# A fused attention and two-MLP kernel: a deeper read-ahead of the second MLP's weights, another order inside a slot, and constant products between the attention steps

## The chip, the cores and the metric

The kernel runs on one core of one Trainium2 chip. The metric is the time on the device in microseconds (us), from the start to the end of one execution; inputs lie in device memory (HBM) before it starts.

## The reference

Four batches, eight heads, 576 positions, head size 64, everything in float32. Attention comes first, causal within a window of 128 positions with a bias that grows with distance; its output, as 2304 tokens of 512 numbers, goes through a first MLP, a root-mean-square norm and a gated second MLP:

```python
scores = scale * np.matmul(q, k.transpose(0, 1, 3, 2))
scores = np.where(mask, scores + bias[None], -1000000000.0)
attn = np.exp(scores - np.max(scores, axis=-1, keepdims=True))
attn = attn / (np.sum(attn, axis=-1, keepdims=True) + 1e-09)
x = np.matmul(attn, v)                      # 2304 x 512 after the heads are put side by side
...
h = x @ w_in                                # 512 x 2048
x = (h * np.clip(h + 3.0, 0.0, 6.0) / 6.0) @ w_out
...
xn = x / np.sqrt(np.mean(x * x, axis=-1, keepdims=True) + 1e-06) * rms_g
g, val = xn @ w_gate, xn @ w_val            # 512 x 1536 each
out = (g / (1.0 + np.exp(-g)) * val) @ w_out
```

The weights of both MLPs are float64 in HBM.

## The kernel before, in words

Tokens are cut into 18 tiles of 128 and the tiles into six blocks of three. Heads are worked on in pairs, so one *pair* is a block and two heads, and one *step* (`Step`) is one tile of 128 queries of a pair against its 256 keys. Scores go through TensorE (`scores`), then VectorE adds the bias and finds the maximum (`bias`), ScalarE takes the exponential (`exp`), GpSimd inverts the sum (the last two lines of `exp`), VectorE multiplies by it (`divide`), TensorE transposes the result (`transpose`), ScalarE copies it out of PSUM (`weights`) and TensorE multiplies with the values (`values`). After a pair's last step `Pair.finish` splits the result into two float32r parts, which is how the MLPs read it. The stages of one step are spread over four positions of a software pipeline: at position `t` the code works on scores, bias and exp of step `t` (`cur`), on the division of step `t-1` (`mid`), on the transposes of step `t-2` (`old`) and on the values of step `t-3` (`done`).

The first `AHEAD` = 15 positions run attention alone (loop at L486), preceded by 50 transposes of a constant (L483). After them come *slots* (loop at L564): in each, one tile of 128 of the first MLP's 2048 hidden numbers is computed for a block (`product1`, 12 matmuls), the activation is applied and split (L586, L587, L592, L597), the attention stream goes on by one step, and the second product (`product2`, called in `finish1`, 9 matmuls) of the slot before is added up. There are 96 slots before the second MLP, in seven parts (`PARTS`); block 0 is split into two parts so that block 1 can come between.

Weights are converted on the chip from float64 words into two float32r parts (`convert`, a generator in six stages on ScalarE and VectorE). The first MLP's 16 units are loaded and converted by `First` in the late steps and in the first 15 slots (parts 0 and 1). The second MLP's 36 tiles go through `Second`: `load` issues the DMA of one raw tile, `begin` does the first three stages of a conversion, `finish` the rest, and the result is stored to a DRAM scratch (`kept`), from which GpSimd's queue fetches it for the second MLP. Raw tiles have two buffers. `finish` is called once a slot in part 3 from its fourth slot on, and in three slots of four in parts 4 and 5.

When a block's last slot is over, `Norm` takes over its three output tiles: `square` (ScalarE and GpSimd) finds the factor `ri`, `front` at the start of a slot multiplies a tile by it and copies the transposes of an earlier tile out of PSUM (`yt`), and `back`, at a slot's end, issues four transposes (`ps_x`) and the next `square`. `ps_x` and the attention's transposes share one PSUM buffer (tag `T`).

Each engine works its instructions off in the order in which the code issues them (`manual_schedule`), so a waiting instruction holds everything behind it on that engine. The DMAs of SP are such a queue too. The lines that matter here, in a slot of the kernel before:

```python
for x in norms:
    x.front()                                  # L568
...
if mid:
    mid.divide()                               # L583
act.activation(r[:, :nq], ps[:, :nq], AF.Relu, bias=three)   # L586
```

and in `Second.finish`:

```python
self.load()                                    # L199
...
self.done += 1
self.begin()                                   # L206
```

Of the kernel before, what the change touches and what calls it, by code (L numbers as in the profile page):

```python
# [14 lines left out]
U64 = mybir.dt.uint64  # L15
# [5 lines left out]
P = 128  # L21
# [3 lines left out]
DM = H * D  # L25
# [12 lines left out]

WARM = 50
PARTS = [(0, 0, CUT), (1, 0, M1), (0, CUT, M1)] + [(b, 0, M1) for b in range(2, len(BLOCKS))]  # L40
# [15 lines left out]
def f32(ap):  # L56
    return ap.bitcast(F32)
# [3 lines left out]
def fused_kernel(ctx: ExitStack, tc: tile.TileContext, qd, kd, v, w1, w2, rms_g, out):  # L61
# [29 lines left out]
    def make_constants():  # L91
        make_identity(nc, ident)

        pool.iota(rel, pattern=[[-1, 2 * P]], base=P, channel_multiplier=1, allow_small_or_imprecise_dtypes=True)
        pool.affine_select(out=rel, in_=rel, compare_op=ALU.is_ge, fill=BIG, base=P, pattern=[[-1, 2 * P]], channel_multiplier=1)
        pool.affine_select(out=rel, in_=rel, compare_op=ALU.is_ge, fill=BIG, base=WINDOW - 1 - P, pattern=[[1, 2 * P]], channel_multiplier=-1)
        pool.memset(half, -0.5)
        pool.memset(minus, -1.0)
        vec.memset(three, 3.0)
        for h in range(H):  # L100
            vec.memset(qscale[h % 2 * D : (h % 2 + 1) * D, h // 2 : h // 2 + 1], -float(2 ** (h + 1)) / np.sqrt(D))
        pool.tensor_copy(rel_split, rel)
        pool.memset(rel_split[HALF:, : P + HALF], BIG)
# [66 lines left out]
    class Second:  # L170


        def __init__(self):
            self.n, self.loaded, self.done, self.raw, self.run = 3 * M2, 0, 0, None, None
            self.kept = [dram.tile([P, 2, 2, DM], F32, tag=f"w2_{i}", name=f"w2_{i}") for i in range(self.n // 2)]
            self.pairs = []

        def load(self):
            i = self.loaded
            self.raw = None  # L180
            if i < self.n:
                self.raw = wcpool.tile([P, DM], U64, tag="w", name="wraw", bufs=2)
                sp.dma_start(out=self.raw, in_=w2[i // 3, :, (i % 3) * DM : (i % 3 + 1) * DM])
                self.loaded += 1

        def begin(self):

            if self.raw is not None:
                self.run = convert(self.raw, DM, wcpool, 1, vec)
                for _ in range(3):  # L190
                    next(self.run)

        def finish(self):

            if self.run is None:
                return
            run, self.run = self.run, None
            next(run)
            self.load()  # L199
            t = wcpool.tile([P, 2, DM], F32R, tag="wt", name="w", bufs=1)  # L200
            run.send(t)
            next(run)
            i = self.done
            sp.dma_start(out=self.kept[i // 2][:, i % 2], in_=f32(t))
            self.done += 1
            self.begin()  # L206

# [212 lines left out]
    class Norm:  # L420
# [24 lines left out]

        def front(self):
            t = self.t
            if t < self.n:
                vec.tensor_scalar(self.y[t], self.y[t], self.ri[t], None, ALU.mult)
            if t - 2 in self.ps:  # L450
                k = t - 2
                yt = ypool.tile([P, KC, P], F32, tag="yt", name="yt", bufs=2)
# [29 lines left out]
    warm = ps_h.tile([P, 4 * P], F32, tag="h", name="warm")  # L482
    for i in range(WARM):  # L483
        pe.transpose(warm[:, i % 4 * P : (i % 4 + 1) * P], ident, ident)
    pairs[0].scale()
    for t in range(AHEAD):  # L486
# [4 lines left out]
        if done:  # L491
            done.values()
        if mid:
            mid.divide()
        if old:
            old.weights()
        cur.bias()
        cur.exp()
        if done and done.last:
            done.pair.finish()  # L500
        prepare(cur)
        if t == 2:
# [45 lines left out]
    for p, (b, m0, m1) in enumerate(PARTS):  # L548
# [15 lines left out]
        for m in range(m0, m1):  # L564
            t, slot = slot, slot + 1
            cur, mid, old, done = [stream.get(t - i) for i in (0, 1, LAG, LAG + 1)]
            for x in norms:
                x.front()  # L568
            if p == 3 and m == 2:
                first.close()  # L570
                wcpool = second.enter_context(tc.tile_pool(name="wcpool", bufs=1, side="right", **OPEN))
                W2.load()
                W2.begin()
            ps = ps_h.tile([P, 4 * P], F32, tag="h", name="ps_h")
# [5 lines left out]
            if done:  # L580
                done.values()
            if mid:
                mid.divide()  # L583
            g = gpool.tile([P, 2, 3 * P], F32R, tag="g", name="g")
# [3 lines left out]
            if old:  # L588
                old.weights()
            if cur:  # L590
                cur.bias()
            act.copy(g[:, 0, :nq], r[:, :nq])  # L592
            if cur:
                cur.exp()
            if done and done.last:
                done.pair.finish()
            vec.tensor_sub(g[:, 1, :nq], r[:, :nq], f32(g[:, 0, :nq]))  # L597
            prepare(cur)
            between(mid)
            if p < 2:  # L600
                k = m + 1 if p == 0 else CUT + 1 + m
                W1.load(k + 3)
                if k < M1:
# [3 lines left out]
                    W1.step(k, 5)  # L607
            if not last and (p == 3 and m > 2 or p > 3 and m % 4 != 3):
                W2.finish()
# [25 lines left out]
    for b, (_, n) in enumerate(BLOCKS2):  # L635
        nq = n * P
        xs, xs2 = xs2, []
        for m in range(M2):
            for x in norms:
                x.front()  # L640
            ps_g = ps_a.tile([P, 4 * P], F32, tag="S0", name="ps_g") if m % 2 else ps_h.tile([P, 4 * P], F32, tag="h", name="ps_g")
# [64 lines left out]
```

## Time and profile before

| | us |
|---|---|
| median of 3 runs | 1069.63 (1067.77 to 1069.94) |
| the profiled execution, its own time | 1070.02 |
| its span, first to last instruction | 1068.1 |
| TensorE busy in the span | 1031.7 (97%) |
| VectorE busy | 459.6 (43%) |
| ScalarE busy | 434.4 (41%) |
| GpSimd busy | 103.8 (10%) |
| granted TensorE clock, mean (1.0 is 2.4 GHz) | 0.971 |

In the profile PE is TensorE's matmuls, PEld its weight loads, DVE VectorE, ACT ScalarE, POOL GpSimd and SP the engine whose queue issues most DMAs. All times inside a profile are counted from the start of the span. PE's busy time is that of records whose ends are modelled, so a stretch with PE busy throughout is not a stretch at PE's peak: the granted clock and the length of equal pieces of work tell more. The whole span has three stages: constants and the 15 attention steps to 55 us, the slots to 609 us, the second MLP to the end.

### The profile page before, as it was taken

How to read it: one execution, taken by the hardware profiler on the slowest of the kernel's cores; microseconds unless marked ns; L12 is line 12 of the kernel's file. 1: busy time of each engine (PE TensorE's matmuls, PEld its weight loads, DVE VectorE, ACT ScalarE, POOL GpSimd, SP SyncE). 2: the span in 40 equal slices, each digit the busy share in tenths (PEclk: the TensorE clock that was granted, in tenths of full speed). 3: DMA queues.
4: the chain of work that ended last, by engine and by line, in shares of the span. 5: the costliest groups of instructions: out<-in, count | busy, mean ns of one | idle time of the engine just before them, and what ended most of it. 6: DMA issues, size and time to landing. Idle time of an engine off the chain costs nothing.

```text
span 1068.1 us, 14589 instructions
## 1 busy us (share of the span) xinstructions
PE 1031.7 (97%) x5678; PEld 895.2 (84%) x5678; DVE 459.6 (43%) x1096; ACT 434.4 (41%) x952; POOL 103.8 (10%) x219
## 2 busy tenths in 40 slices
PE   7899999999999799989999999999999999999998
PEld 5477778888777588878899899999999999999997
DVE  3578774345576666767632322212212222222212
ACT  3679864355555556656532332112112112112111
POOL 2322011121111111111121010000000000000000
PEclk7599999999999999999999999999999999999999
DMA  6154500003565455444459720010100100100000
GB/s 207 55 212 185 224 28 28 29 29 97 188 202 192 166 166 186 163 165 142 145 193 305 250 71 11 11 49 1 60 1 1 60 1 1 60 1 1 30 1 30
DMA packets 49237, 105.28 MB, mean 99 GB/s; under 512 B 3856, under 2 KB 28432, under 8 KB 44816
## 3 DMA queue, kind: packets, MB, share of 16 engines
q1 hardware_dynamic: 46576, 85.47, 23.8%
q0 software_dynamic: 2592, 18.88, 5.2%
q8 instruction: 44, 0.72, 0.3%
q14 instruction: 25, 0.20, 0.1%
HBM read 76.02 MB, written 28.31 MB: 98 GB/s over the span
## 4 chain that ended last, share of the span: by engine, by line
PE 55%; ACT 0%; issue 0%; DVE 0%; ACTq 0%
PE ps_o L412 20%; PE ps_g L399 14%; PE ps_v L399 14%; PE ps_h L399 6%; PE ps_av L355 0%; PE ps_t L342 0%; PE ps_x L465 0%; PE ps_s L293 0%; DVE y L632 0%; ACT wx L123 0%; DVE xs L541 0%; ACT xs L540 0%; ACT junk L441 0%; ACT t L586 0%; DVE t L587 0%
## 5 line engine op out<-in xcount | busy, mean ns | idle before, releaser
L412 PE MATMUL ps_o<-w,g 128*128 128x512 f32 x1512 | 390.9, 402 | 5.7 <-DVE w L134 2.9
L412 PEld LDWEIGHTS ps_o<-w,g 128*128 128x128 f32 x1512 | 279.5, 190 | 71.6 <-issue 9.6
L399 PE MATMUL ps_h<-xs,w 128*128 128x384 f32 x1152 | 222.8, 341 | 7.9 <-DVE t L587 7.6
L399 PEld LDWEIGHTS ps_h<-xs,w 128*128 128x128 f32 x1152 | 205.0, 190 | 18.4 <-DVE t L587 11.7
L647 DVE TENSOR_TENSOR t<-t,ps_v 128x384 f32<-128x384 f32 x72 | 39.9, 554 | 306.0 <-PE ps_v L399 306.0
L399 PE MATMUL ps_g<-xs,w 128*128 128x384 f32 x864 | 163.8, 337 | 0.5 <-ACT xs L540 0.3
L399 PE MATMUL ps_v<-xs,w 128*128 128x384 f32 x864 | 161.6, 334 | 0.0
L399 PEld LDWEIGHTS ps_g<-xs,w 128*128 128x128 f32 x864 | 153.1, 188 | 7.4 <-ACT xs L540 0.7
L399 PEld LDWEIGHTS ps_v<-xs,w 128*128 128x128 f32 x864 | 151.0, 188 | 0.0
L644 ACT ACTIVATE t<-ps_g 128x384 f32<-128x384 f32 x72 | 35.4, 492 | 196.6 <-PE ps_g L399 196.6
L649 ACT CAST g<-t 128x384 fp32r<-128x384 f32 x72 | 36.9, 513 | 156.6 <-DVE t L647 156.6
L586 ACT ACTIVATE t<-ps_h,three 128x384 f32<-128x384 f32 x96 | 55.3, 576 | 103.3 <-PE ps_h L399 102.9
L587 DVE SCALAR_TENSOR_TENSOR t<-t,ps_h 128x384 f32<-128x384 f32 x96 | 52.9, 551 | 85.1 <-ACT t L586 85.1
L328 ACT ACTIVATE t<-t,m 128x256 f32<-128x256 f32 (+1 forms) x144 | 69.4, 483 | 27.2 <-DVE m L316 27.2
L592 ACT CAST g<-t 128x384 fp32r<-128x384 f32 x96 | 49.4, 514 | 44.3 <-DVE t L587 42.4
L597 DVE TENSOR_TENSOR g<-t,g 128x384 fp32r<-128x384 f32 x96 | 53.4, 556 | 26.0 <-ACT g L592 25.7
L342 PE MATMUL ps_t<-ident,t 128*128 128x128 f32 x272 | 50.0, 310 | 12.8 <-ACT yt L453 8.7
L134 DVE TENSOR_TENSOR w<-wx,w 128x512 fp32r<-128x512 f32 (+1 forms) x52 | 44.5, 857 | 34.2 <-ACT w L132 34.2
L330 POOL TENSOR_SCALAR r<-den 128x2 f32<-128x2 f32 x72 | 21.7, 301 | 386.0 <-ACT t L328 386.0
L336 DVE TENSOR_SCALAR t<-t,r 128x256 f32<-128x256 f32 (+1 forms) x144 | 42.4, 337 | 39.0 <-POOL r L331 37.3
L132 ACT CAST w<-wx 128x512 fp32r<-128x512 f32 (+1 forms) x52 | 39.1, 751 | 47.1 <-issue 27.0
L650 DVE TENSOR_TENSOR g<-t,g 128x384 fp32r<-128x384 f32 x72 | 40.2, 558 | 41.7 <-ACT g L649 41.7
(63 smaller groups left out, 742.4 us busy)
## 6 DMA issues: line engine op xcount, KB each, us to landing
wraw<-w SPq DMA_DIRECT2D x36, 512.0 KB, 4.4
w<-w SPq DMA_DIRECT2D x36, 512.0 KB, 3.2
w<-w POOLq DMA_DIRECT2D x18, 1024.0 KB, 5.3
wraw<-w SPq DMA_DIRECT2D x16, 1024.0 KB, 7.8
kraw<-kd SPq DMA_DIRECT2D x20, 256.0 KB, 2.7
vraw<-v SPq DMA_DIRECT2D x20, 256.0 KB, 4.0
qraw<-qd SPq DMA_DIRECT2D x24, 192.0 KB, 2.9
x<-yt SPq DMA_DIRECT2D x18, 256.0 KB, 2.7
```

What stands on the lines that cost most here:

```text
L134: vec.tensor_sub(t[:, 1], x, f32(t[:, 0]))
L328: act.activation(p, p, AF.Exp, bias=self.m[:, a : a + 1], scale=-1.0, accum_out=self.den[:, a : a + 1])
L336: vec.tensor_scalar(p, p, self.r[:, a : a + 1], None, ALU.mult)
L342: pe.transpose(self.ps[:, a, c], self.t[:, a, c * P : (c + 1) * P], ident)
L399: pe.matmul(ps[:, : n * P], lhsT=w[:, a, c * P : (c + 1) * P], rhs=xs[c][:, b, : n * P], start=(k == 0), stop=(k == 3 * KC - 1),)
L412: pe.matmul(o, lhsT=g[:, a, i * P : (i + 1) * P], rhs=w[:, b], start=(m == first and a == 0 and b == 0), stop=(m == last and a == 1),)
L586: act.activation(r[:, :nq], ps[:, :nq], AF.Relu, bias=three)
L587: vec.scalar_tensor_tensor(out=r[:, :nq], in0=r[:, :nq], scalar=6.0, in1=ps[:, :nq], op0=ALU.min, op1=ALU.mult)
L592: act.copy(g[:, 0, :nq], r[:, :nq])
L597: vec.tensor_sub(g[:, 1, :nq], r[:, :nq], f32(g[:, 0, :nq]))
L647: vec.tensor_mul(r[:, :nq], r[:, :nq], ps_v[:, :nq])
L650: vec.tensor_sub(g[:, 1, :nq], r[:, :nq], f32(g[:, 0, :nq]))
```

## The change

1. The 50 transposes of the identity at the start become five products of 256 columns on the constant `rel` (`busy(WARM)`), and GpSimd makes `rel` ahead of the identity. One more such product stands in each of the 15 steps, behind `values` (`busy(1)`). Their result is never read.
2. In a step, `bias` comes ahead of the division of the step before, and `exp` last; `Pair.finish` comes ahead of both.
3. In a slot, the division comes behind the activation's second operation and the copy of the transposes; `Pair.finish` and the last part of the split come ahead of `exp`.
4. `Norm.front` is cut in two: `store` stays at the slot's start, `scale` goes behind `exp` to the slot's end.
5. `Second` keeps a list of raw tiles: two are loaded at the start (part 3, slot 2), the first `begin` is one slot later, and each `finish` loads the tile after next. In `finish`, the next tile's `begin` comes ahead of the last conversion stage. `finish` starts a slot later.

```diff
-WARM = 50
+WARM = 5
...
     def make_constants():
-        make_identity(nc, ident)
         pool.iota(rel, ...
         pool.affine_select(out=rel, ...
         pool.affine_select(out=rel, ...
+        make_identity(nc, ident)
...
         def load(self):
             i = self.loaded
-            self.raw = None
             if i < self.n:
-                self.raw = wcpool.tile([P, DM], U64, tag="w", name="wraw", bufs=2)
-                sp.dma_start(out=self.raw, in_=w2[i // 3, :, (i % 3) * DM : (i % 3 + 1) * DM])
+                raw = wcpool.tile([P, DM], U64, tag="w", name="wraw", bufs=2)
+                sp.dma_start(out=raw, in_=w2[i // 3, :, (i % 3) * DM : (i % 3 + 1) * DM])
+                self.raw.append(raw)
                 self.loaded += 1
         def begin(self):
-            if self.raw is not None:
-                self.run = convert(self.raw, DM, wcpool, 1, vec)
+            if self.raw:
+                self.run = convert(self.raw.pop(0), DM, wcpool, 1, vec)
...
             run.send(t)
+            self.begin()
             next(run)
             i = self.done
             sp.dma_start(out=self.kept[i // 2][:, i % 2], in_=f32(t))
             self.done += 1
-            self.begin()
...
-    for i in range(WARM):
-        pe.transpose(warm[:, i % 4 * P : (i % 4 + 1) * P], ident, ident)
+    def busy(n):
+        for _ in range(n):
+            pe.matmul(warm[:, : 2 * P], lhsT=rel[:, :P], rhs=rel, start=True, stop=True)
+    busy(WARM)
...
         if done:
             done.values()
-        if mid:
-            mid.divide()
+        busy(1)
         if old:
             old.weights()
         cur.bias()
-        cur.exp()
         if done and done.last:
             done.pair.finish()
+        if mid:
+            mid.divide()
+        cur.exp()
         prepare(cur)
...
-            for x in norms:
-                x.front()
             if p == 3 and m == 2:
...
                 W2.load()
-                W2.begin()
+                W2.load()
+            for x in norms:
+                x.store()
...
-            if mid:
-                mid.divide()
             act.activation(r[:, :nq], ps[:, :nq], AF.Relu, bias=three)
             vec.scalar_tensor_tensor(out=r[:, :nq], ...
             if old:
                 old.weights()
+            if mid:
+                mid.divide()
+            act.copy(g[:, 0, :nq], r[:, :nq])
             if cur:
                 cur.bias()
-            act.copy(g[:, 0, :nq], r[:, :nq])
-            if cur:
-                cur.exp()
             if done and done.last:
                 done.pair.finish()
             vec.tensor_sub(g[:, 1, :nq], ...
+            if cur:
+                cur.exp()
+            for x in norms:
+                x.scale()
...
-            if not last and (p == 3 and m > 2 or p > 3 and m % 4 != 3):
+            if p == 3 and m == 3:
+                W2.begin()
+            if not last and (p == 3 and m > 3 or p > 3 and m % 4 != 3):
                 W2.finish()
```

How the issued order moves, first on VectorE in the steps. Here `t<-t,r` (L336) is the division, the two `ISA t,m` (L316) are the bias of one step, `qraw` (L249) is a scaling that every third step has. Before:

```order
L336 TENSOR_SCALAR t<-t,r 128x256 x2
L316 ISA t,m<-ps_s_255,rel 128x256
L316 ISA m 128x1
L316 ISA t,m<-ps_s_256,rel 128x256
L316 ISA m 128x1
L336 TENSOR_SCALAR t<-t,r 128x256 x2
L316 ISA t,m<-ps_s_284,rel 128x128
```

and now:

```order
L316 ISA t,m<-ps_s_212,rel 128x256
L316 ISA m 128x1
L316 ISA t,m<-ps_s_213,rel 128x256
L316 ISA m 128x1
L336 TENSOR_SCALAR t<-t,r 128x256 x2
L316 ISA t,m<-ps_s_242,rel 128x128
L316 ISA m 128x1
L316 ISA t,m<-ps_s_243,rel 128x128
L316 ISA m 128x1
L336 TENSOR_SCALAR t<-t,r 128x256 x2
```

The rows look alike, but the division that stands behind a step's bias now is that of the step before, where it stood ahead of it.

Second, VectorE in a slot of part 4 that has a norm and a conversion: `y<-y,ri` is the norm's scaling, `t<-t,ps_h` the activation's second operation, `xs` the end of `Pair.finish`, `g<-t,g` the split, and `wx`, `wy`, `w` are the stages of a conversion (`wy<-wraw` the first to read a loaded tile, `w<-wx,w` the last). Before:

```order
L449 TENSOR_SCALAR y<-y,ri 128x512
L336 TENSOR_SCALAR t<-t,r 128x256 x2
L587 SCALAR_TENSOR_TENSOR t<-t,ps_h 128x384
L316 ISA t,m<-ps_s_3735,rel_split 128x256
...
L270 TENSOR_TENSOR xs_3764<-ps_av,xs_3764 128x384
L597 TENSOR_TENSOR g<-t,g 128x384
L130 SCALAR_TENSOR_TENSOR wx<-wx,wy 128x512
L134 TENSOR_TENSOR w<-wx,w 128x512
L120 TENSOR_SCALAR wy<-wraw 128x512
L127 TENSOR_SCALAR wy<-wraw 128x512
```

and now:

```order
L592 SCALAR_TENSOR_TENSOR t<-t,ps_h 128x384
L336 TENSOR_SCALAR t<-t,r 128x256 x2
L316 ISA t,m<-ps_s_3694,rel_split 128x256
...
L270 TENSOR_TENSOR xs_3717<-ps_av,xs_3717 128x384
L602 TENSOR_TENSOR g<-t,g 128x384
L449 TENSOR_SCALAR y<-y,ri 128x512
L130 SCALAR_TENSOR_TENSOR wx<-wx,wy 128x512
L120 TENSOR_SCALAR wy<-wraw 128x512
L127 TENSOR_SCALAR wy<-wraw 128x512
L134 TENSOR_TENSOR w<-wx,w 128x512
```

The scaling has gone from the first place to the seventh row shown, and the next tile's reading from behind the last conversion stage to ahead of it.

Third, SP's queue in part 3 from the norm's last store of the block before (`x_5`) on; `wraw<-w` (L183, now L182) is a raw tile of the second MLP, `w_0` a store of a converted one. Before:

```order
L456 DMA x_5_2543<-yt 128x512
L183 DMA wraw<-w 128x512
L456 DMA x_0_2685<-yt 128x512
L238 DMA kraw<-kd 128x512
L240 DMA qraw<-qd 128x384
L242 DMA vraw<-v 128x4x128
L183 DMA wraw<-w 128x512
L204 DMA w_0_105<-w 128x1024
```

and now:

```order
L458 DMA x_5_2513<-yt 128x512
L182 DMA wraw<-w 128x512 x2
L458 DMA x_0_2651<-yt 128x512
L238 DMA kraw<-kd 128x512
L240 DMA qraw<-qd 128x384
L242 DMA vraw<-v 128x4x128
L458 DMA x_1_2721<-yt 128x512
L182 DMA wraw<-w 128x512
L205 DMA w_0_105<-w 128x1024
```

The second raw tile is issued ahead of the next pair's `kraw`, `qraw` and `vraw` where it stood behind them, and the third a slot's store earlier than its conversion begins.

## Rows read from the trace of the kernel before

**Rows 1.** Windows by stage: length, busy of each engine (instructions), granted clock, DMA share, GB/s.
```profile
9.54:55.29 45.75, 37.26 (x185) 21.70 (x185) 23.05 (x94) 26.42 (x77) 13.88 (x28) 0.54 0.33 109
55.29:112.25 56.96, 55.69 (x327) 43.48 (x325) 47.23 (x107) 48.98 (x95) 15.37 (x24) 0.98 0.52 192
...
142.33:267.34 125.01, 124.87 (x728) 101.63 (x726) 61.78 (x176) 61.74 (x160) 22.37 (x48) 1.00 0.15 46
267.34:474.59 207.25, 190.19 (x1116) 156.36 (x1114) 137.75 (x353) 121.10 (x284) 28.67 (x65) 0.96 0.54 179
```
**Rows 2.** Timeline of the start: start, length, engine, line, operation, [idle before <- what ended it].
```profile
2.15 0.40 POOL L96 TENSOR_SCALAR_AFFINE_SELECT rel<-rel 128x256 f32<-128x256 f32 x1
...
3.85 0.42 DVE L249 TENSOR_SCALAR qraw<-qraw,qscale 128x384 f32<-128x384 f32 x1 [2.25 <-DMA qraw<-qd]
...
9.54 1.90 PE L302 MATMUL ps_s<-kraw,qraw 64*128 64x128 f32 x12
```
**Rows 3.** Windows of L484 (the transposes at the start) alone: PE, PEld, granted clock.
```profile
1.35:6.69 5.34, 5.34 (x25) 5.34 (x26) 1.00 0.92 258
6.69:9.50 2.81, 2.81 (x27) 2.69 (x25) 1.00 0.74 301
```
**Rows 4.** Timeline of the steps: the chain from one step's exp to the next.
```profile
13.52 0.51 ACT L328 ACTIVATE t<-t,m 128x256 f32<-128x256 f32 x1 [2.11 <-DVE m L316]
...
15.75 0.62 DVE L336 TENSOR_SCALAR t<-t,r 128x256 f32<-128x256 f32 x2 [1.92 <-POOL r L331]
...
16.74 0.51 ACT L328 ACTIVATE t<-t,m 128x256 f32<-128x256 f32 x1 [1.88 <-DVE m L316]
```
**Rows 5.** Timeline of PE: scores of two steps, scores and next product of the first slot.
```profile
38.68 1.23 PE L302 MATMUL ps_s<-kraw,qraw 64*128 64x256 f32 x4
...
41.94 1.23 PE L302 MATMUL ps_s<-kraw,qraw 64*128 64x256 f32 x4
...
59.12 0.70 PE L302 MATMUL ps_s<-kraw,qraw 64*128 64x256 f32 x4
...
60.93 1.32 PE L399 MATMUL ps_h<-xs,w 128*128 128x384 f32 x6
```
**Rows 6.** Timeline of a stall: a raw tile's issue, its first reader, PE's next work.
```profile
266.12 0.50 SPq L183 DMA_DIRECT2D wraw<-w  x1
...
266.98 0.60 PE L465 MATMUL ps_x<-ident,y 128*128 128x128 f32 x4
...
271.10 0.67 ACT L123 ACTIVATE wx<-wraw 128x512 f32<-128x512 f32 x1 [3.35 <-DMA wraw<-w]
...
272.30 0.66 PE L342 MATMUL ps_t<-ident,t 128*128 128x128 f32 x4 [2.60 <-ACT yt L453]
```
**Rows 7.** Waits of the whole span: total us, times, longest.
```profile
ACT wx L123 <- DMA wraw<-w: 21.2, 12, 3.6
...
DVE y L449 <- POOL ri L444: 15.8, 16, 2.2
```
**Rows 8.** Timeline: PE in a slot with a norm, a pair's end and a conversion.
```profile
470.09 0.66 PE L342 MATMUL ps_t<-ident,t 128*128 128x128 f32 x4 [3.01 <-ACT yt L453]
```
**Rows 9.** Windows of single slots and, last, of four undisturbed ones (columns as in Rows 1).
```profile
267.34:277.34 10.00, 7.40 (x37) 5.82 (x35) 5.22 (x11) 4.97 (x10) 0.66 (x1) 0.83 0.63 214
294.05:301.21 7.16, 5.35 (x30) 4.24 (x28) 3.95 (x10) 3.45 (x10) 0.92 (x2) 1.00 0.96 316
318.63:334.01 15.38, 13.10 (x68) 10.64 (x69) 10.27 (x26) 9.25 (x22) 1.31 (x4) 0.89 0.65 211
344.81:352.17 7.36, 5.57 (x34) 4.45 (x33) 3.65 (x10) 3.16 (x10) 1.00 (x2) 1.00 0.94 306
352.17:360.58 8.41, 6.72 (x40) 4.82 (x40) 6.01 (x12) 4.91 (x11) 0.74 (x2) 1.00 0.39 133
366.80:378.18 11.38, 8.32 (x35) 6.93 (x36) 6.89 (x21) 6.60 (x18) 2.87 (x7) 0.72 0.49 166
464.17:474.59 10.42, 7.40 (x36) 6.06 (x36) 6.38 (x19) 6.71 (x18) 2.56 (x6) 0.84 0.52 177
401.25:423.57 22.32, 22.32 (x140) 18.77 (x138) 15.88 (x43) 13.94 (x34) 2.90 (x7) 1.00 0.53 176
```

More of the change, by code (lines that the diff above doesn't have):

```diff
@@ L173, in __init__ @@
         def __init__(self):
-            self.n, self.loaded, self.done, self.raw, self.run = 3 * M2, 0, 0, None, None
+            self.n, self.loaded, self.done, self.raw, self.run = 3 * M2, 0, 0, [], None
             self.kept = [dram.tile([P, 2, 2, DM], F32, tag=f"w2_{i}", name=f"w2_{i}") for i in range(self.n // 2)]
@@ L444, in square, with scale @@
                 pool.tensor_tensor(self.ri[k], ss, half, ALU.pow)
-        def front(self):
+        def scale(self):
             t = self.t
@@ L449, in front, with store @@
                 vec.tensor_scalar(self.y[t], self.y[t], self.ri[t], None, ALU.mult)
-            if t - 2 in self.ps:
-                k = t - 2
+        def store(self):
+            k = self.t - 2
+            if k in self.ps:
                 yt = ypool.tile([P, KC, P], F32, tag="yt", name="yt", bufs=2)
@@ L639, in fused_kernel @@
             for x in norms:
-                x.front()
+                x.store()
+                x.scale()
             ps_g = ps_a.tile([P, 4 * P], F32, tag="S0", name="ps_g") if m % 2 else ps_h.tile([P, 4 * P], F32, tag="h", name="ps_g")
```

## The prediction, made before the changed kernel ran

> **What bounds the kernel now.** I read the windows by stage first [rows 1]. From 142 to 267 us, in plain slots, PE is busy for 124.87 of 125.01 us at full clock: that stage is bound by PE, and so is the second MLP behind it; a change of order can give nothing there. Three stages differ. In the 15 steps (45.75 us) the granted clock is 0.54, that is 1.2 GHz nearly throughout, and no engine is full. In the first slots ScalarE and VectorE are at 86% and 83% with the weights' conversion, and PE is covered. From 267 to 475 us PE has 17 us without work and a clock of 0.96.
>
> Next, the timeline in each of these. In the steps, exp begins at 13.52, the division that needs its sum ends at 16.37 (15.75 and 0.62), and the next exp, which stands behind that division and a bias in VectorE's queue, begins at 16.74 [rows 4]: 3.22 us a step through three engines, and 45.75 / 15 is 3.05. So the steps run at the latency of one chain. PE alone would need 3.26 us for a full step at 1.2 GHz (scores to scores, 38.68 to 41.94) and 1.81 at 2.4 GHz (59.12 to 60.93, the same three pieces in the first slot) [rows 5]; every third step has half the work.
>
> In the late stage, the raw tile issued at 266.12 is first read at 271.10, and ScalarE stands for 3.35 us at the head of its queue; PE, needing a copy from behind it, is idle for 2.60 [rows 6]. Such waits add up to 21.2 us in 12 places on ScalarE [rows 7]. The other long PE gaps there, 3.01 us at 470, end on the norm's copy out of PSUM [rows 8], in slots where VectorE first waits for the norm's factor (15.8 us in 16 places [rows 7]). Four undisturbed slots take 22.32 us, 5.58 each [rows 9]: what a slot takes above that is what can be won.
>
> **The change, part by part.** The sum is made against the profiled execution's 1070.02 us (span 1068.1 and 1.9 around it), 0.4 above the median of the runs.
>
> *The start.* The 50 transposes end at 9.5 and the scores start behind them at 9.54, while their operand is ready at 4.27 [rows 2]. 25 transposes of 128 columns take 5.34 us and 27 the next 2.81 [rows 3]: 0.214 us each, then 0.104. The profile's 1.00 for the first 6.7 us is therefore no reading; PE ran there at 1.2 GHz and rose at 6.69, having done nothing but transposes. A float32 product of 256 columns is two passes, or 4 x 0.214 = 0.85 us at 1.2 GHz and 0.42 at 2.4; the far end is a pair of scores of that width, 1.23 and 0.70 [rows 5]. I take the stream's price, since these products too are issued back to back. `rel` is ready at 2.55 now [rows 2] and earlier when made first, say 2.1. Five products end at 2.1 + 4.3 = 6.4 (at most 2.55 + 6.15 = 8.7). **-3.1 us.**
>
> *The steps.* With the bias ahead of the last step's division, a step no longer waits for its predecessor's sum: the 3.22 us chain, with transposes and copy added to it, is spread over two steps, so it can't hold a step below about 2. ScalarE has 26.42 / 15 = 1.76 us of work a step, VectorE 1.54 [rows 1], PE 1.81 + 0.42 = 2.23 at 2.4 GHz. PE becomes the largest; I add 0.17 for what queues in order lose: 2.4 a step, 36.0 in all. **-9.75 us.** This stands on PE at full clock. Every fall seen in the slots came after PE had stood idle for over 2 us [rows 6, 8], and those slots show 0.83 and 0.84 [rows 9], and the added product leaves PE with 2.2 of 2.4 us taken. Between 2.1 and 2.6 a step the term is -14.2 to -6.75.
>
> The row and the Trainium skill differ here. The row shows PE's rate doubling at 6.69 after transposes alone [rows 3]. The Trainium skill, TensorE: Matmul & The Clock Gate, Part 4: PE-mode transpose, says that the full clock doesn't engage for transposes, as they don't count as PE being busy. By that rule a third of a step's PE work would not keep the clock, and the sum would be that of the first rival; by the row it is this one. The trace disagrees with the rule for a run of transposes, and no run here shows it for a mix.
>
> *The first 15 slots.* The exchange of exp, `Pair.finish` and the split changes the order of the same work on two engines that are 14 and 17% idle: nothing, within 4 us either way (ScalarE's idle 8 us halved [rows 1]).
>
> *The read-ahead.* Now a raw tile has one slot (5.58 us) more than the 4.98 us it took from issue to first reader [rows 6], so that reader finds it landed; what the slot hid before, it hides still. The slots that lie on such a wait cost 10.00 (of which 0.6 is the norm's transposes [rows 6], which stay), 7.16, 15.38 for two, and 7.36 [rows 9], less 5.58 for each of the five: 3.8 + 1.6 + 4.2 + 1.8. **-11.4 us**, the two stretches at half clock that follow the waits included. The earlier `begin` inside `finish` puts 0.9 us of VectorE's work into a wait on ScalarE and adds none. The DMAs stay 36; the second tile's passes ahead of one pair's three loads, for which I add nothing.
>
> *The norm's scaling and the slot's order.* The scaling moves to where its factor is a slot old, and `Pair.finish` no longer stands behind two exps. The three slots concerned cost 8.41, 11.38 and 10.42, less 5.58 each and 0.6 for transposes in each [rows 9]: 2.2 + 5.2 + 4.2 = 11.6. They also carry the conversion, and ScalarE has some 6.6 us of work in the two long ones, above PE's 6.2, so they can't shrink to nothing. Bounds are 0 and 11.6; I take two thirds, as most of the 3 us idle is waiting and not work. **-7.8 us.** What is late next there is ScalarE itself.
>
> Sum: -3.1 - 9.75 - 11.4 - 7.8 = -32.05, so 1070.0 - 32 = **1038 us**. Its own range, with the terms' ends (steps at 2.1 and -4 in the first slots and the norm's whole 11.6; steps at 2.6 and +4 and a third of the norm's), is 1024 to 1049.
>
> **The rivals.**
>
> *The clock stays at 1.2 GHz in the steps.* For: in the steps now PE has records over 37.26 of 45.75 us and 0.54 [rows 1], so being busy with this mix did not raise it. Between the fifth product and the first division PE also has to wait once, for one chain of some 2.9 us [rows 4], with two scores and two products in it. Against: the added products are 128 by 128 streams, and the start and the slots rise on such. Then PE needs 3.26 + 0.85 in a full step; over three steps, with half work in one, some 9.0 + 2.55 = 11.5, or 57.7 us in all, where now it is 45.75: the products would cost more than the shorter chain gives. 1070 - 3.1 + 11.9 - 11.4 - 7.8 = **1060**. Chance 0.25.
>
> *The read-ahead hides nothing new.* If SP's queue holds the load until its buffer's last reader is done in the slot where the tile is needed, the waits stay: 1038 + 11.4 = **1049**. Against: the buffer's readers are in `begin`, a slot earlier in the queues. Chance 0.08.
>
> *Exp at the end of the slot delays the conversion behind it (slower).* Before, the division was done while VectorE waited for the activation; now it stands between the activation's second operation and the bias, so exp starts up to 0.62 us later [rows 4], and the conversion's copies on ScalarE stand behind both. Of one exp (0.51) more, that is 0.62 to 1.13, mean 0.87, in each of the 15 + 36 slots that convert: +44, so **1082**. It decides from 32 / 51 = 0.63 us a slot on. For: both queues are in order, and in the first slots they are over 80% full. Against: in the four undisturbed slots, three of which convert, ScalarE works 13.94 of 22.32 us [rows 9], room enough for a later start. Chance 0.05.
>
> **How the numbers follow.** The forecast has 0.62. The range holds 8 in 10 when it reaches from the forecast's lower end, 1024, to the first rival at 1060, which takes in the second. A measurement can tell about 0.2%, 2.1 us, from no change. The forecast and two rivals are faster; I leave 0.01 for a mix of them that ends level and share the third between level (0.01) and slower (0.04): 0.94, 0.02, 0.04.
>
> **What would show it right or wrong.** Right: the first scores before 7 us, the first slot's product at 41 to 45, a granted clock above 0.8 from there back to the start; no wait of ScalarE on a raw tile over 0.5 us from 260 us on; no slot of parts 3 to 5 over 8 us; VectorE's wait for the norm's factor gone. Wrong in the steps: a clock near 0.5 and PE covered throughout, with the first slot's product after 60. Wrong in the slots: plain slots longer than 5.58 us with ScalarE idle before exp. Lengths of the slots from 142 to 267 and of the second MLP must not change.

## The result, and the profile after

The changed kernel takes 1027.34 us (median of 4 runs, 1026.62 to 1027.63) against 1069.79 of the kernel before on the same chip: a ratio of 0.9604 (95% interval 0.9587 to 0.9620), 42 us less. The prediction was 1038 with a range of 1024 to 1060: the sign and the range held, and the gain was 10 us larger than the sum. One run below, of the kernel with two products at the start, took 1222.33 us at a mean clock of 0.754 and is left out of that kernel's ratio. The profiled execution has a span of 1025.9 us and a mean granted clock of 1.000 in place of 0.971.

The stages of the changed kernel, cut at the same places of the program as in [rows 1] (columns as there; the last row is all that comes behind slot 67):

```profile
6.67:41.05 34.38, 31.25 (x216) 17.82 (x215) 23.57 (x99) 26.81 (x79) 14.87 (x29) 1.00 0.49 167
41.05:125.53 84.48, 80.54 (x465) 63.55 (x466) 70.81 (x139) 72.08 (x124) 20.73 (x23) 1.00 0.52 195
125.53:250.40 124.87, 124.86 (x728) 101.69 (x726) 58.47 (x174) 62.00 (x159) 22.53 (x46) 1.00 0.16 50
250.40:432.39 181.99, 180.27 (x1116) 151.44 (x1114) 136.78 (x353) 121.37 (x284) 35.17 (x64) 1.00 0.60 196
432.39:1025.90 593.51, 589.21 (x3144) 542.68 (x3142) 166.71 (x326) 153.65 (x311) 22.66 (x44) 1.00 0.20 67
```

The first slot's product starts at 41.05 where it was 55.29: 14.2 us come from the start and the steps. Slots 0 to 13 take 84.48 where they took 87.04 (55.29 to 142.33): 2.6. The plain slots are the same (124.87 and 125.01). The late slots take 181.99 for 207.25: 25.3, and PE is idle there for 1.7 us in place of 17. From 432.39 on the length is 593.51, the same as from 474.59 on before. So nearly all of the 42 us come from two places, the start with the steps and the late slots; the first slots gave little.

The start and the first steps, PE alone (timeline: start, length, engine, line, operation, [idle before <- what ended it]), which answer to [rows 2, 3]:

```profile
2.17 4.57 PE L488 MATMUL warm<-rel 128*128 128x256 f32 x10 [2.17 <-POOL rel L95]
6.67 0.49 PE L302 MATMUL ps_s<-kraw,qraw 64*128 64x128 f32 x4
7.09 0.70 PE L488 MATMUL warm<-rel 128*128 128x256 f32 x2
7.72 0.70 PE L302 MATMUL ps_s<-kraw,qraw 64*128 64x256 f32 x4
8.36 0.70 PE L488 MATMUL warm<-rel 128*128 128x256 f32 x2
8.99 0.70 PE L302 MATMUL ps_s<-kraw,qraw 64*128 64x256 f32 x4
10.13 0.53 PE L342 MATMUL ps_t<-ident,t 128*128 128x128 f32 x2 [0.44 <-DVE t L336]
```

Five products take 4.5 us, and the scores start at 6.67, not 9.54. The wait for the first division, where I expected one chain of 2.9 us, is 0.44. But a product between scores takes 0.63 us from its start to that of the scores behind it (7.09 to 7.72), not the 0.42 I took.

ScalarE's exps of four steps in a row, which answer to [rows 4]:

```profile
17.77 0.52 ACT L328 ACTIVATE t<-t,m 128x256 f32<-128x256 f32 x1
...
20.29 0.42 ACT L328 ACTIVATE t<-t,m 128x128 f32<-128x128 f32 x1
...
23.22 0.51 ACT L328 ACTIVATE t<-t,m 128x256 f32<-128x256 f32 x1 [0.83 <-DVE m L316]
...
25.44 0.51 ACT L328 ACTIVATE t<-t,m 128x256 f32<-128x256 f32 x1
```

From exp to exp it is 2.5, 2.9 and 2.2 us, on average 34.38 / 15 = 2.29, for 3.05 before.

Single slots of the changed kernel, in the order of [rows 9] and for the same slots (the third row is two slots, the last one four undisturbed ones):

```profile
250.40:256.02 5.62, 5.62 (x36) 4.81 (x35) 3.39 (x9) 3.64 (x8) 1.23 (x2) 1.00 0.64 192
272.75:277.94 5.19, 5.19 (x31) 4.43 (x30) 4.34 (x11) 4.23 (x9) 1.08 (x2) 1.00 1.01 320
294.61:305.92 11.31, 11.31 (x70) 9.43 (x69) 9.89 (x23) 7.94 (x19) 1.59 (x4) 1.00 0.79 256
316.71:322.11 5.40, 5.40 (x34) 4.65 (x33) 4.19 (x10) 3.88 (x8) 1.12 (x2) 1.00 1.04 330
322.11:328.23 6.12, 6.12 (x41) 5.00 (x39) 5.39 (x14) 4.50 (x11) 0.74 (x2) 1.00 0.63 216
334.10:340.64 6.54, 5.79 (x38) 4.93 (x37) 5.13 (x15) 4.87 (x14) 2.38 (x5) 1.00 0.53 181
425.58:432.39 6.81, 5.85 (x39) 4.95 (x37) 5.29 (x15) 4.88 (x14) 2.22 (x4) 1.00 0.60 203
363.48:385.79 22.31, 22.31 (x139) 18.77 (x138) 15.69 (x41) 13.88 (x33) 3.67 (x7) 1.00 0.52 170
```

The first four rows (five slots), which lay on a wait for a raw tile, are PE-bound now: 27.5 us for 39.9. The three with the norm take 19.5 for 30.2, and only the two long ones keep some PE idle time:

```profile
337.71 0.66 PE L342 MATMUL ps_t<-ident,t 128*128 128x128 f32 x4 [0.76 <-ACT yt L455]
...
429.44 0.66 PE L342 MATMUL ps_t<-ident,t 128*128 128x128 f32 x4 [0.96 <-ACT yt L455]
```

The second is the wait of 3.01 us of [rows 8], in the same slot, a third as long; the first was 3.06. In the list of waits, ScalarE's on the raw tiles (21.2 us [rows 7]) is gone altogether; VectorE's for the norm's factor is down from 15.8 us in 16 places to three:

```profile
DVE y L449 <- POOL ri L444: 3.1, 3, 1.1
```

### The profile page after: what moved, and what is told of

Read it like the earlier page. It is cut to its first block, busy times and chain, and to the rows that moved or that the text cites. A ratio compares the mean times of both kernels' runs of the same rounds, so it can differ in the third digit from the quotient of the medians.

```text
span 1025.9 us, 14621 instructions
## 1 busy us (share of the span) xinstructions
PE 1010.6 (99%) x5668; PEld 880.3 (86%) x5668; DVE 457.2 (45%) x1096; ACT 437.2 (43%) x952; POOL 118.4 (12%) x219
## 4 chain that ended last, share of the span: by engine, by line
PE 57%; DVE 1%; DMA 0%; ACT 0%; issue 0%; ACTq 0%; DVEq 0%
PE ps_o L412 21%; PE ps_g L399 15%; PE ps_v L399 15%; PE ps_h L399 6%; PE ps_av L355 1%; PE ps_t L342 0%; DMA w<-w 0%; PE ps_x L467 0%; PE ps_s L293 0%; DVE w L134 0%; DVE wx L130 0%; DVE t L592 0%; ACT t L591 0%; DVE wy L120 0%; ACT junk L441 0%
## 5 line engine op out<-in xcount | busy, mean ns | idle before, releaser
L412 PE MATMUL ps_o<-w,g 128*128 128x512 f32 x1512 | 386.2, 399 | 3.9 <-DVE w L134 2.1
L412 PEld LDWEIGHTS ps_o<-w,g 128*128 128x128 f32 x1512 | 276.5, 188 | 68.3 <-issue 9.4
L399 PE MATMUL ps_h<-xs,w 128*128 128x384 f32 x1152 | 219.6, 338 | 0.1
L659 DVE TENSOR_TENSOR t<-t,ps_v 128x384 f32<-128x384 f32 x72 | 39.9, 554 | 306.0 <-PE ps_v L399 306.0
L328 ACT ACTIVATE t<-t,m 128x256 f32<-128x256 f32 (+1 forms) x144 | 69.7, 486 | 13.6 <-DVE m L316 13.1
L330 POOL TENSOR_SCALAR r<-den 128x2 f32<-128x2 f32 x72 | 34.1, 474 | 335.9 <-ACT t L328 335.9
L331 POOL TENSOR_TENSOR r<-r,minus 128x2 f32<-128x2 f32 x72 | 57.1, 794 | 6.0
L342 PE MATMUL ps_t<-ident,t 128*128 128x128 f32 x272 | 44.4, 283 | 4.8 <-ACT t L328 2.6
```

Source lines behind the costliest of these rows:

```text
L328: act.activation(p, p, AF.Exp, bias=self.m[:, a : a + 1], scale=-1.0, accum_out=self.den[:, a : a + 1])
L331: pool.tensor_tensor(self.r, self.r, minus, ALU.pow)
L342: pe.transpose(self.ps[:, a, c], self.t[:, a, c * P : (c + 1) * P], ident)
L399: pe.matmul(ps[:, : n * P], lhsT=w[:, a, c * P : (c + 1) * P], rhs=xs[c][:, b, : n * P], start=(k == 0), stop=(k == 3 * KC - 1),)
L412: pe.matmul(o, lhsT=g[:, a, i * P : (i + 1) * P], rhs=w[:, b], start=(m == first and a == 0 and b == 0), stop=(m == last and a == 1),)
L659: vec.tensor_mul(r[:, :nq], r[:, :nq], ps_v[:, :nq])
```

## The experiments

Each kernel below is the changed one with one thing altered. They ran in three groups, each on one chip beside runs of the kernel before, to which the ratios are. The changed kernel itself was run once more, with the last group:

> The changed kernel itself once more, on the chip of the three above: its time there is what they are compared with; 0.960 of the kernel before, the first product within 1 us of 41.05.

Measured: 1027.20 us, ratio 0.9598 (0.9583 to 0.9612), the first slot's product at 40.17 where the profile above has 41.05. For the kernels of its own group (the old start, the small products, the three orders undone at once) differences are direct; for the others they are the difference of their ratio to 0.9598, times the 1071 us of the kernel before. Each of the two ratios has a half-width of 1.6 us, so a difference under 2.2 us is not told from none. Lengths of stages are read from one profiled execution of each kernel.

These executions differ among themselves. In four of them (the changed kernel run again, no products, no read-ahead, three orders undone) the clock fell for 3.4 us in slot 12. The slot in the second profile of the changed kernel:

```profile
112.30:119.42 7.12, 5.46 (x22) 4.26 (x21) 5.75 (x8) 4.97 (x6) 0.00 (x0) 0.89 0.27 115
```

PE was idle there for 0.90 and 0.76 us ahead of the fall; in the first profile gaps of 0.92 and 0.76 us at the same place were followed by none, and the slot took 6.41. Slots 0 to 13 take 85.05 with this fall and 84.5 without it. And the first long norm slot (6.54 above) took 7.48 and 7.35 us in two kernels whose slots are the changed kernel's, so a difference under 1 us in that slot tells nothing.

### The steps: products or order

```diff
             done.values()
-        busy(1)
```

> The changed kernel without the 15 products between the steps; the five at the start stay. Theory A (the products hold the clock): the granted clock falls to 0.5 in the steps, a step takes 3.0 us as PE's work at 1.2 GHz (9.0 us for three steps), the first slot's product comes at 50 to 53 us instead of 41.05 and the whole takes 1036 to 1040 us. Rival B (the new order alone packs the steps densely enough): the clock stays at 1.0, PE has 15 x 0.42 = 6.3 us less to do, the first product comes at 35 to 39 us and the whole takes 1021 to 1026 us.

Measured: 1028.64 us, ratio 0.9598 (0.9583 to 0.9612), the same as the changed kernel; the first product at 42.54. Neither theory held as it stood. The clock did fall, twice in the steps, for 6.8 us each, and the mean clock of the span is 0.992 or 0.993 in all four executions. Windows of this kernel (columns as before; the last is the whole stage):

```profile
8.00:11.00 3.00, 1.45 (x10) 0.84 (x8) 2.06 (x12) 1.97 (x8) 1.68 (x4) 1.00 0.58 195
11.10:17.90 6.80, 6.59 (x32) 3.71 (x32) 3.39 (x17) 4.71 (x16) 2.35 (x7) 0.50 0.90 342
18.00:34.90 16.90, 11.31 (x98) 6.88 (x98) 13.00 (x49) 14.49 (x41) 7.16 (x13) 1.00 0.36 111
35.00:41.80 6.80, 6.65 (x32) 4.17 (x32) 4.57 (x20) 4.36 (x13) 3.27 (x7) 0.50 0.12 35
6.70:42.54 35.84, 28.24 (x185) 17.15 (x184) 23.54 (x98) 26.21 (x77) 14.84 (x29) 0.81 0.46 158
```

It fell after a stretch in which PE worked 1.45 of 3 us, was back at 18 with PE covered, and stayed up for 17 us with PE busy for two thirds. The products hold the clock, then, but they cost PE 15 x 0.63 = 9.5 us, and what they save and what they cost are nearly level: the stage takes 35.8 us from the first scores to the first slot's product, where the changed kernel's two profiles have 34.4 and 34.2, and what follows is as long as there. Some 1.5 us may be their worth, less than the ratios can tell and no more than this stage varies in the other profiles with the same steps (33.9 to 35.3).

```diff
         busy(1)
+        if mid:
+            mid.divide()
         if old:
             old.weights()
         cur.bias()
+        cur.exp()
         if done and done.last:
             done.pair.finish()
-        if mid:
-            mid.divide()
-        cur.exp()
```

> The changed kernel with the old order in the steps (division ahead of the bias, exp ahead of Pair.finish), the products kept. Theory (the order breaks the chain): a step takes 3.0 to 3.2 us again whatever the clock, the first slot's product comes at 51 to 54 us, the whole takes 1037 to 1041 us if the products hold the clock, and with the clock at 0.5 some 64 us and 1050. Rival (the clock alone gave the gain, the chain was slow because its PE pieces were): the first product stays within 2 us of 41 and the whole within 3 us of 1027.

Measured: 1040.03 us, ratio 0.9706 (0.9690 to 0.9722): 11.6 us slower than the changed kernel. In the profile the stage is 13.4 us longer than the changed kernel's 34.38 and the rest as long as there (984.6 and 984.8), which the intervals allow. The whole stage in one window:

```profile
6.74:54.54 47.80, 38.74 (x216) 21.41 (x215) 24.21 (x100) 26.76 (x79) 14.23 (x29) 0.82 0.37 121
```

A step takes 3.19 us, the chain of [rows 4], at a clock of 0.82: three falls, products and all. So it is the order that made the steps short. The clock needs both, the order and something in the products' place: with the products alone it is 0.82, with the order alone 0.81.

```diff
             done.values()
-        busy(1)
+        for i in range(4):
+            pe.transpose(warm[:, i * P : (i + 1) * P], ident, ident)
```

> The changed kernel with four transposes of the identity (4 x 0.104 us at 2.4 GHz, the same streaming time) in place of each product between the steps. Theory (PE's streaming time holds the clock, transposes included): the clock stays at 1.0 from its rise on, first slot's product at 40 to 43 us, the whole within 2 us of the changed kernel. Rival (transposes don't count): the clock falls in the steps as in the kernel without products, and as PE has more to do then, the first product comes at 44 to 50.

Measured: 1027.56 us, ratio 0.9597 (0.9582 to 0.9611), the first product at 40.80, and over the steps:

```profile
6.74:40.80 34.06, 30.66 (x246) 19.70 (x245) 23.54 (x99) 26.78 (x79) 14.88 (x29) 1.00 0.51 172
```

The clock is 1.00 throughout, with no product in the steps, while without either it was 0.81 over the same stage (the last window of the kernel without products). The scores of 256 columns take 0.70 us from 7.75 to 35.98, their length at 2.4 GHz, and the mean clock of the span is 1.000 in all four executions. These float32 transposes hold it as the products do.

### The start

```diff
-WARM = 5
+WARM = 50
...
-    busy(WARM)
+    for i in range(WARM):
+        pe.transpose(warm[:, i % 4 * P : (i % 4 + 1) * P], ident, ident)
```

(the identity is made ahead of `rel` again)

> The changed kernel with the 50 transposes at the start (and the identity made first) as before; the products between the steps stay. Theory (the start's term adds): scores at 9.5 us instead of 6.67, the first slot's product at 43.5 to 44 and the whole 2.5 to 3.1 us slower than the changed kernel. Rival (the first steps wait for something else, so that an earlier start gains less): 0 to 1.5 us slower.

Measured: 1030.27 us, ratio 0.9628 (0.9612 to 0.9643), 3.1 us slower than the changed kernel run again. The scores start at 8.64 (6.00 there), the first product at 42.52 (40.17). The term adds, but the start's own share is 2.4 us, not 3.1: most of the rest is the first long norm slot of the profiled execution, 7.35 us for 6.55, which has nothing to do with the start. The scores behind the transposes, and those of the next kernel, behind two products:

```profile
8.64 0.49 PE L302 MATMUL ps_s<-kraw,qraw 64*128 64x128 f32 x4
```

```profile
4.31 0.80 PE L302 MATMUL ps_s<-kraw,qraw 64*128 64x128 f32 x4
```

The same four matmuls ran at 2.4 GHz in the first row and at 1.2 in the second.

```diff
-WARM = 5
+WARM = 2
```

> The changed kernel with two products at the start in place of five. Theory (the scores wait for the products alone): scores at 4.3 us, where their operand is ready, instead of 6.67, and if the clock rises at the same time the first product at 38.5 to 39.5 and the whole 1.5 to 2.5 us faster than the changed kernel. Rival (PE then idles in the first steps and the clock rises later or falls): the first product at 41 to 48.

Measured: 1027.0 us, ratio 0.9588 (0.9572 to 0.9604), not to be told from the changed kernel. Scores at 4.31, yet the first product at 40.48, between the two profiles of the changed kernel (41.05 and 40.17): the granted clock rises only at 10.26 (a product before that takes 1.14 us and one after it 0.63), so the first scores, products and transposes ran at 1.2 GHz. What is saved ahead of the scores is mostly paid behind them.

```diff
-WARM = 5
+WARM = 2
...
-        busy(1)
+        pe.matmul(warm[:, :P], lhsT=rel[:, :P], rhs=rel[:, :P], start=True, stop=True)
```

> The changed kernel with two products at the start and products of half the width (128 columns, 0.21 us at 2.4 GHz) between the steps. Theory (PE is full in the steps): PE has 15 x 0.21 = 3.2 us less to do and the first product comes at 37 to 39 us, 2 to 4 us earlier, if the clock holds. Rival (ScalarE and the chain hold the steps, or the clock falls): the first product at 40 to 43.

Measured: 1025.12 us (1024.62 to 1028.26), ratio 0.9586 (0.9562 to 0.9610); the first product at 39.16 against 40.17. Its median is 2.1 us under that of the changed kernel run again, but the runs overlap: the lowest median of all, and not shown to be faster. The steps themselves are no shorter, 34.89 us from the first scores at 4.27, of which some 7 run at 1.2 GHz, against 34.17. PE then waits for more, mostly on ScalarE, so PE is not the only bound of the steps by then.

### The read-ahead

```diff
                 W2.load()
-                W2.load()
+                W2.begin()
...
             run.send(t)
-            self.begin()
             next(run)
...
             self.done += 1
+            self.begin()
...
-            if p == 3 and m == 3:
-                W2.begin()
-            if not last and (p == 3 and m > 3 or ...
+            if not last and (p == 3 and m > 2 or ...
```

> The changed kernel with the raw tiles loaded as before: one tile ahead, begin at finish's end and in slot 2 of part 3. Theory (the read-ahead removes the waits on the DMA): ScalarE's waits on raw tiles come back at some 20 us in all, the slots at the places of before take 7 to 10 us again, the clock falls once or twice, and the whole takes 1037 to 1040 us. Rival (the new slot order covers the waits, the read-ahead adds little): below 1031 us.

Measured: 1041.93 us, ratio 0.9732 (0.9710 to 0.9755): 14.4 us slower. This also undoes the order of `begin` inside `finish`, which is tried alone below. The waits are back, 12 as before and nearly as long in all, and so are the slots (the same first four rows as above):

```profile
ACT wx L123 <- DMA wraw<-w: 20.8, 12, 4.1
```

```profile
251.44:262.66 11.22, 8.67 (x37) 6.75 (x35) 6.67 (x14) 5.48 (x11) 1.33 (x2) 0.70 0.56 190
279.41:285.76 6.35, 5.35 (x30) 4.24 (x28) 2.84 (x7) 2.68 (x7) 0.92 (x2) 1.00 0.95 317
302.51:318.21 15.70, 12.98 (x69) 10.78 (x68) 10.21 (x26) 8.87 (x21) 1.28 (x4) 0.89 0.63 202
329.03:335.46 6.43, 5.57 (x34) 4.46 (x32) 2.54 (x6) 2.35 (x6) 0.96 (x2) 1.00 0.96 318
```

The new slot order doesn't cover them: these five slots take 39.7 us, and before it was 39.9. The two long norm slots grow too, to 9.16 and 7.91. But the profiled execution, 1046.23 us with a mean clock of 0.992, is the slowest of the four; the others have 0.996 or 0.997 and 1041.10 to 1042.12 us, so up to 4 us of these lengths may be that execution's own.

### The slot's order and the norm

The scaling at the slot's start again:

```diff
             for x in norms:
+                x.scale()
                 x.store()
...
-            for x in norms:
-                x.scale()
```

> The changed kernel with the norm's scaling at the slot's start again (ahead of the copy out of PSUM), all else kept. Theory (the wait for the norm's factor cost most of the norm slots): VectorE waits 0.7 us and more again in 9 places, the three slots of before (2.3, 4.8 and 3.6 us longer) get half or more of that back, the whole takes 1032 to 1038 us. Rival (the place of Pair.finish and exp, or the read-ahead's rest, made these slots short): within 2 us of 1027.

Measured: 1029.41 us, ratio 0.9608 (0.9593 to 0.9622): level. VectorE's wait for the factor is back, 18.1 us in 14 places, and the two long norm slots take 7.42 and 7.51 for 6.54 and 6.81. The rival, by the time; the wait is back, but it costs 1.6 us at most in the two slots together.

The old order of the other pieces:

```diff
+            if mid:
+                mid.divide()
             g = gpool.tile(...)
...
             if old:
                 old.weights()
-            if mid:
-                mid.divide()
-            act.copy(g[:, 0, :nq], r[:, :nq])
             if cur:
                 cur.bias()
+            act.copy(g[:, 0, :nq], r[:, :nq])
+            if cur:
+                cur.exp()
             if done and done.last:
                 done.pair.finish()
             vec.tensor_sub(g[:, 1, :nq], ...
-            if cur:
-                cur.exp()
```

> The changed kernel with the slot's order of before (division ahead of the activation, bias and exp ahead of Pair.finish, exp ahead of the split); the norm's scaling stays at the slot's end and the read-ahead stays. Theory (Pair.finish ahead of exp shortens the three long norm slots): these slots, now 6.12, 6.55 and 6.81 us, take 1 to 3 us more each, the clock may fall once, and the whole is 3 to 9 us slower than the changed kernel. Rival 1 (the place of begin inside finish did it): within 2 us of the changed kernel. Rival 2 (the old order is better in the first 15 slots, where the division was done while VectorE waited): these slots shorten by 0.1 to 0.4 us each.

Measured: 1030.89 us, ratio 0.9628 (0.9612 to 0.9644), 3.2 us slower. The long norm slots take 7.62 and 7.41, and slots 0 to 13 take 85.54, where they take 84.48 to 84.54 in all eight profiles with the new order and no fall of the clock in them. So my slower rival went the other way: the new order makes the converting slots a little shorter.

`begin` behind the last conversion stage again, the loads a tile further ahead kept (the diff is the second and third piece of the read-ahead's):

> The changed kernel with the next tile's begin behind the last conversion stage again, read-ahead and orders kept. Theory (begin fills VectorE's wait on ScalarE): VectorE's wait for ScalarE's copy, 9.2 us in all now, goes back to some 34; where a slot is bound by these two engines (norm slots) it takes 0.5 to 1.5 us more, the whole 1 to 4 us slower than the changed kernel. Rival (no slot is bound there): within 1 us.

Measured: 1028.34 us, ratio 0.9604 (0.9590 to 0.9619): level. VectorE's wait for ScalarE's copy is 34.5 us in all, as expected, the long norm slots take 7.21 and 7.27, hardly outside their spread, and no other slot shows it.

Undone singly each of the three costs 0 to 3 us, and the three norm slots together had become 10.7 shorter. The last kernel undoes all three at once:

> The changed kernel with all three orders of the slots undone at once (scaling at the start, division, bias, exp and Pair.finish as before, begin behind the last conversion stage); the loads a tile further ahead, the steps and the start stay. Undone singly each gave the two long norm slots (6.55 and 6.81 us) 0.5 to 1.1 us. Theory A (their costs add up): these slots take 9.2 and 8.8, the whole is 5 to 8 us slower than the changed kernel. Theory B (any one of them hides the others' waits, so that only all three together show the gain): 10 to 11.4 us each with a fall of the clock, the whole 9 to 13 us slower. Theory C (the loads alone shortened them): below 8 us each, the whole 2 to 4 us slower.

Measured: 1038.53 us, ratio 0.9704 (0.9690 to 0.9719), 11.3 us slower than the changed kernel run again. The three norm slots and PE's wait in the last of them:

```profile
323.21:331.01 7.80, 6.61 (x40) 4.73 (x38) 5.92 (x12) 4.29 (x10) 0.74 (x2) 1.00 0.69 236
337.25:347.67 10.42, 7.37 (x36) 6.09 (x36) 6.32 (x19) 6.60 (x18) 2.83 (x7) 0.84 0.51 171
433.40:443.81 10.41, 7.39 (x35) 6.10 (x36) 6.38 (x19) 6.70 (x18) 2.56 (x6) 0.84 0.54 181
```

```profile
439.31 0.72 PE L342 MATMUL ps_t<-ident,t 128*128 128x128 f32 x4 [3.02 <-ACT yt L455]
```

The costs do not add, as theory B has it. Undone singly, the two long slots grew by 1.6, 1.7 and 1.1 us together; undone at once, by 7.5, and the clock falls once in each. With any two of the three orders in place PE waits 1.4 to 1.8 us for ScalarE's copy out of PSUM; with none of them 3.0, as in the kernel before. That one order alone would do, as theory B says, is not shown: none was left alone. Nor do the falls seem to be the main cost: one of the four runs has a mean clock of 0.998 where the others have 0.995, and still took 1037.92 us.

## Why the prediction was right, and where its sizes were off

**The start** was forecast at -3.1. The scores start 2.9 us earlier (9.54 to 6.67; 3.5 in the second profile), and undoing it moves the first slot by 2.4 and the whole by 3.1.

**The steps** were forecast at 2.4 us each, -9.75, and came to 2.29 us each, -11.4; undoing the order alone costs 11.6 by the ratios and 13.4 by the profile. The mechanism held: the division behind the next step's bias takes the three-engine chain out of the step. But the sum rested on "This stands on PE at full clock" with the products as what keeps it, and there the reason was half right. The products do keep the clock and yet are worth 1.5 us at most, not told from nothing, because each costs 0.63 us in its place where I took the streaming price of 0.42; the far end of my own bounds, 0.70, was the nearer one. That 2.29 is so near 2.4 is partly luck: PE's records are 2.08 us a step, under my 2.23 in spite of the dearer product, since my sum took a full step's work for all 15, where some have half and the first ones have no transposes or values yet. PE idles for 0.44 us at the first division, and not for a chain's length; without the products it is 1.55, so they fill most of that.

**The first rival**, the clock at 1.2 GHz in the steps, did not come about. On the Trainium skill's statement (TensorE: Matmul & The Clock Gate, Part 4: PE-mode transpose) that the full clock doesn't engage for transposes: for the float32 transposes of this kernel the runs disagree (the Trainium skill's measurement there is of bf16). Four transposes in each product's place left the granted clock at 1.00 over the stage, and with nothing in their place it was 0.81. And in the run with the old start the first scores, behind fifty transposes and nothing else, take 0.49 us, the length of the changed kernel's at 2.4 GHz, where in the kernel with two products ahead of them they take 0.80. A whole stage of transposes alone was not tried. What the prediction says of the falls, that each came after PE had stood idle for over 2 us, is true of the late slots of the kernel before (2.28 to 3.06 us) and not of the changed kernel, where gaps of 0.90 and 0.76 us came ahead of one.

**The first 15 slots** were put at nothing within 4 us: 2.6, of which 1.5 is slot 0 (4.10 for 5.64 us), whose first matmuls no longer run at 1.2 GHz.

**The read-ahead** was forecast at -11.4 by the five slots that lay on a wait; these slots gave 39.9 - 27.5 = 12.4, and undoing it costs 14.4, as the long norm slots also grow when a raw tile is late. The second rival (nothing new is hidden) fell: not one wait of ScalarE on a raw tile is left.

**The norm's scaling and the slot's order** is the term that failed in size: -7.8 forecast, 10.7 in the three slots, 11.3 by undoing all of it. The step that failed is "ScalarE has some 6.6 us of work in the two long ones, above PE's 6.2, so they can't shrink to nothing". The 6.6 us were ScalarE's busy time in a window of 11.4 us [rows 9], which held parts of the neighbours' work (the exps of the step before, for one); a slot of the changed kernel has 4.87 and 4.88 of ScalarE in 6.54 and 6.81, below PE's 5.8. The upper bound, 11.6, was nearly the value. The two thirds were a guess between the bounds, and no run bears them out.

**The third rival** (exp at the slot's end delays the conversion) was wrong in sign: the old order makes slots 0 to 13 1.1 us longer.

By stages, which add, the two profiled spans differ by 42.2 us: 2.9 up to the first scores (forecast 3.1), 11.4 in the steps (9.75), 2.6 in slots 0 to 13 (0), 0.1 in the plain slots (0) and 25.3 in the late ones (19.2). Of the late ones 12.4 are the five slots of the read-ahead (11.4), 10.7 the three of the norm (7.8) and 2.1 their neighbours, for which nothing was forecast. So the missing 10 us are about 6 in the late slots, 2.6 in the first ones and 1.6 in the steps.

The costs of undoing, 3.1, 11.6, 14.4 and 11.3, come to 40.4, but they are no such sum: the order of `begin` is undone in both of the last two, and costs here were seen not to add.

The lower end of the prediction's own range is added up wrong: its terms give 1070.0 - 44.3 = 1025.7, not 1024. The measured 1027.3 lies inside either. Of the signs named, the first scores (6.67), the clock, the waits on raw tiles and the longest late slot (6.81) came as said; the wait for the norm's factor is 3.1 us in three places and not gone, and the first slot's product is at 41.05 in one profile and 40.17, just ahead of the 41 to 45, in the other.

## What to carry to other kernels

When a stage runs at the latency of a chain through several in-order engines, moving one operation behind the next iteration's independent work can shorten every iteration: with the products in both, the order took a step from 3.19 to 2.29 us here. Price a slot's possible gain by its length above an undisturbed slot, and don't take an engine's busy time in a stretched window for that slot's own work. And undo related edits together as well as singly: three orders that cost 0 to 3 us apiece when undone cost 11 together, since any two of them kept PE's wait under 2 us.

## What the runs showed of the hardware that was not expected

A float32 product of 128 by 128 by 256 takes 0.85 us behind its like at 1.2 GHz (4.5 us for five), but 0.63 at 2.4 GHz between scores, where its like back to back take 0.43 (in the second profile of the changed kernel). The product of half the width takes 0.42 there, also 0.2 more than half of that; the cause is open. And a lower clock was nearly free where PE wasn't the bound: without the products 13.6 us of the steps ran at 1.2 GHz, and the stage took 35.8 us for 34.4 and 34.2.
